# Attention on 32 memory slots, then a mixture of experts: the queries are transposed on TensorE, the first two batches are worked on in halves

## The chip, the cores and the metric

The kernel runs on one core of one Trainium2 chip, in float32. The metric is the device time of one execution in microseconds (us). One program does everything: attention first, then the expert network, then the output.

## The reference

There are 8 batches, 8 heads, 576 positions, head size 64, and M = 32 memory slots for each head. The attention works on those slots:

```python
a = exp(phi - phi.max(axis=2)); a /= a.sum(axis=2) + 1e-9        # phi: [8, 8, 576, 32]
k_m = einsum('bhsm,bhsd->bhmd', a, k)                           # 32 pooled keys for each head
v_m = einsum('bhsm,bhsd->bhmd', a, v)
scores = q @ k_m.T / 8; attn = softmax(scores)                  # over the 32 slots
x = (attn @ v_m) as rows of [8 * 576, 512]                      # heads side by side
```

The expert network routes all 4608 rows to 32 slots (8 experts with 4 slots each) by `logits = x @ moe_phi`:

```python
d = softmax(logits, over the 4608 rows); slot_input = d.T @ x
for e in range(8):
    slot_out[e] = relu(slot_input[e] @ w1[e]) @ w2[e]           # w1[e]: 512x1024, w2[e]: 1024x512
c = softmax(logits, over the 32 slots); out = c @ slot_out      # [4608, 512]
```

So 33 MB of q, k, v and phi are read, then 33.5 MB of w1 and w2, and 9.4 MB are written. No row of `slot_input` is final before the last row of all batches has its logits.

## The kernel before

**How the order comes about.** All work is handed to `Plan.add(engine, cost, fn, r=, w=, ...)` with an estimated duration. `Plan.order` then places the operations one after another on five queues (TensorE `PE`, VectorE `DVE`, ScalarE `ACT`, GpSimd `POOL`, and `SP`, which issues every DMA), by these estimates and by the priorities that `plan.at` sets. What comes out is a fixed order on each engine; on the chip each engine goes through its own queue in order, and waits where a semaphore is not there yet. `Slots` are pools of buffers inside one large SBUF tile, the `arena`; a tile of a pool becomes free when its last user is done.

**The attention** goes over four pairs of batches (`bp`), and in a pair over `c` = 0 to 3, two heads each.

- `pool_phi` loads phi of one batch, takes its maximum over the positions (DVE L511, a transposition on PE L519, DVE L524, a broadcast on PE L533, ACT L544), subtracts it on POOL (L549), takes exp on ACT (L555), adds up the nine position blocks on POOL (L562, four instructions that halve the blocks), folds the two halves of the partitions with one small product on PE (L572, with `maskhp`), and takes the reciprocal on DVE (L579, L580).
- `pool_kv` loads k and v of the batch and forms k_m and v_m in PSUM (`kvbank`) with 72 products (L599), whose operands are 64 rows by 32 columns, so that eight tiles of the array work side by side. ACT scales them (L615, L622). The keys are written into zeroed tiles `kps` in two 32-row blocks, and four transpositions on PE (L635) turn them into `kd`; L640, L645 and L662 do the same for the values and multiply them by moe_phi, which gives `vpb`.
- `q_blocks`: DVE transposes q in blocks of 32x32, straight from the loaded tile, in two instructions for each batch (L700). This is why the keys are needed in two blocks: each score is a sum of two products over 32 rows.
- `scores`: 8 products for each `c` (L716, 64x64 tiles, 288 columns) into `scbank`; DVE transposes them back (L730).
- `softmax` of each `c`: DVE maximum (L746), POOL subtraction (L751), ACT exp (L756), DVE sum (L761), ACT, DVE reciprocal (L770), POOL product (L774), DVE transposition (L777); `logits` on PE (L785). When the four `c` of a pair are done, DVE writes the pair's logits `L` (L955).
- `route` of each pair forms that pair's share of `slot_input` (L803 to L922; on PE L810, L821, L849, L875, L881, L909).

When the last pair is routed, DVE joins the four shares and writes `SIM`, the `slot_input` (L969 to L1000). POOL clears the tile `hT` for the hidden layer (L1046) shortly before that.

**The experts.** w1 and w2 come in 32 tiles of 1 MB each (`load_w`). Their buffers `ws` are 19 slots that lie over the arena: a slot can be loaded only when all attention buffers under it are done. PE multiplies (L1064 with w1, L1113 with w2), then come a sum `sr` (L1194 to L1207), 36 products L1220 with the rows' weights `cT`, copies on ACT and DVE (L1229, L1231), and 12 stores of 768 KB (L1239).

**Loads and fillers.** SP issues all loads at L458, in one queue; `FIRST` lists the first nine in order. phi, k and v have two buffers each (`phis`, `kvs`), q has two (`qs`, outside the arena). PE also gets filler products that compute nothing needed (L476, `NWARM` 40 of them at most in the first 25 us of the plan, `NTAIL` 12 around the end of the attention).

## Time and profile before

| | |
|---|---|
| three runs | 224.52, 222.32, 224.25 us, median 224.25 |
| the profiled execution | 221.83 us, of which the span from first to last instruction is 220.1 |
| busy in the span | PE 172.5 us, DVE 135.5, POOL 86.7, ACT 71.4 |
| moved by DMA | 76.45 MB, mean 347 GB/s |
| fillers on PE (L476) | 92 instructions, 25.4 us busy |
| pairs done (start of L955) | first at 62.7 us, last at 135.8 |

A float32 product is two MATMUL instructions in the trace, a transposition on PE is one. A row of the windows gives, for a stretch of the span, the busy time of each engine with the number of instructions, then the granted TensorE clock (1.00 is full speed), the mean busy share of the DMA engines (which reads up to 1.09 when they are saturated) and the GB/s that they moved. A row of the timeline gives start, length, engine, line and operation, and in brackets how long the engine had been idle and what released it.

### The profile page before, as it was taken

The numbers are of one execution on the slowest core, as the hardware profiler recorded it, in microseconds if no ns is written. First come the engines' busy times: TensorE is split into PE (matmuls) and PEld (weight loads), VectorE is DVE, ScalarE is ACT, GpSimd is POOL, SyncE is SP. The second block draws the span as 40 slices with busy tenths as digits, with TensorE's granted clock in tenths as the row PEclk, the third lists the DMA queues.
The fourth block names the chain that finished last, engine by engine and source line by source line (L and its number), as shares of the span: only waits on it lengthen the run. The fifth ranks groups of instructions, "written<-read, shape, count | busy, mean of one in ns | idle before, by whom it ended". The sixth has DMA issues, their size and how long they took to land.

```text
span 220.1 us, 5624 instructions
## 1 busy us (share of the span) xinstructions
PE 172.5 (78%) x2418; PEld 105.3 (48%) x2418; DVE 135.5 (62%) x230; ACT 71.4 (32%) x182; POOL 86.7 (39%) x85
## 2 busy tenths in 40 slices
PE   8997977695798988598988799629999975599400
PEld 6676745354564654356654387415554340065100
DVE  6825048969459999879658965499102860268500
ACT  2041234542516626337342340201002331168400
POOL 6298019596934992999623641030000000000000
PEclk9999999979699999999969999976999999769755
DMA  6999999999999999999596493999999998049997
GB/s 215 383 395 390 380 392 381 390 380 390 385 388 389 388 406 380 389 392 406 194 410 212 188 420 102 401 350 327 395 413 410 408 409 320 3 179 411 415 415 295
DMA packets 27881, 76.45 MB, mean 347 GB/s; under 512 B 1744, under 2 KB 5840, under 8 KB 27856
## 3 DMA queue, kind: packets, MB, share of 16 engines
q1 hardware_dynamic: 27856, 76.09, 91.1%
q8 instruction: 19, 0.31, 0.6%
q14 instruction: 6, 0.05, 0.1%
HBM read 66.65 MB, written 9.44 MB: 346 GB/s over the span
## 4 chain that ended last, share of the span: by engine, by line
PE 41%; DMA 22%; DVE 14%; POOL 9%; issue 5%; ACT 2%; SPq 1%; DVEq 0%; POOLq 0%
DMA top<-in_q_dram 10%; DMA arena<-in_moe_w_dram 9%; PE bank L1064 7%; PE kvbank L476 6%; PE bank L785 5%; PE scbank L716 4%; PE bank L1220 4%; PE kvbank L599 3%; DMA out_dram<-arena 3%; DVE arena L700 3%; POOL arena L774 3%; POOL arena L562 3%; PE bank L849 2%; PE kvbank L1113 2%; POOL arena L751 2%
## 5 line engine op out<-in xcount | busy, mean ns | idle before, releaser
L549 POOL TENSOR_TENSOR arena<-arena 128x1152 f32<-128x1152 f32 x8 | 21.0, 2632 | 16.0 <-ACT arena L544 13.3
L476 PE MATMUL kvbank<-ones 128*128 128x256 f32 x92 | 25.4, 419 | 2.2 <-ACT arena L622 1.1
L700 DVE STREAM_TRANSPOSE arena<-top 128x1152 f32<-128x1152 f32 x16 | 21.7, 1361 | 7.1 <-DMA top<-in_q_dram 7.1
L774 POOL TENSOR_TENSOR arena<-arena,ssm 128x576 f32<-128x576 f32 x16 | 18.5, 1162 | 15.6 <-DVE ssm L770 15.5
L562 POOL TENSOR_TENSOR arena<-arena 128x128 f32<-128x128 f32 (+2 forms) x32 | 23.4, 731 | 2.3 <-ACT arena L555 0.3
L716 PE MATMUL scbank<-arena 64*64 64x288 f32 x256 | 21.6, 433 | 3.0 <-DVE arena L730 2.5
L785 PE MATMUL bank<-arena 128*128 128x288 f32 x64 | 21.4, 464 | 2.6 <-DVE arena L777 2.6
L751 POOL TENSOR_TENSOR arena<-arena,smx 128x576 f32<-128x576 f32 x16 | 18.4, 1158 | 11.5 <-DVE smx L746 11.5
L599 PE MATMUL kvbank<-arena 64*32 64x128 f32 x1152 | 20.2, 273 | 2.2 <-issue 1.5
L476 PEld LDWEIGHTS kvbank<-ones 128*128 128x128 f32 x92 | 18.1, 207 | 6.7 <-issue 1.6
L511 DVE TENSOR_REDUCE arena<-arena 128x128 f32<-128x1152 f32 x8 | 17.0, 2138 | 5.6 <-DMA arena<-in_phi_dram 5.6
L599 PEld LDWEIGHTS kvbank<-arena 64*32 64x32 f32 x1152 | 16.2, 106 | 6.3 <-issue 3.9
L1064 PE MATMUL bank<-arena,SIM 128*32 128x256 f32 x256 | 16.4, 421 | 3.4 <-DVE SIM L1000 3.4
L1113 PE MATMUL kvbank<-arena 128*32 128x512 f32 x128 | 15.6, 598 | 2.9 <-DMA arena<-in_moe_w_dram 2.9
L730 DVE STREAM_TRANSPOSE arena<-scbank 128x576 f32<-128x576 f32 x16 | 12.2, 765 | 8.9 <-PE scbank L716 8.9
L785 PEld LDWEIGHTS bank<-arena 128*128 128x128 f32 x64 | 12.1, 206 | 8.1 <-DVE arena L777 3.8
L1220 PE MATMUL bank<-sr,cT 128*128 128x512 f32 x36 | 13.2, 505 | 3.1 <-DVE sr L1207 1.4
L1231 DVE COPY arena<-bank 128x512 f32<-128x512 f32 x18 | 11.8, 691 | 4.7 <-DMA out_dram<-arena 2.4
L777 DVE STREAM_TRANSPOSE arena<-arena 128x576 f32<-128x576 f32 x16 | 12.1, 758 | 3.8 <-POOL arena L774 3.7
L716 PEld LDWEIGHTS scbank<-arena 64*64 64x64 f32 x256 | 9.0, 137 | 10.8 <-DVE arena L730 4.5
L756 ACT ACTIVATE arena<-arena 128x576 f32<-128x576 f32 x16 | 11.0, 688 | 8.4 <-POOL arena L751 8.4
L1064 PEld LDWEIGHTS bank<-arena,SIM 128*32 128x32 f32 x256 | 8.6, 121 | 10.7 <-DVE SIM L1000 3.6
(104 smaller groups left out, 234.4 us busy)
## 6 DMA issues: line engine op xcount, KB each, us to landing
arena<-in_moe_w_dram SPq DMA_DIRECT2D x32, 1024.0 KB, 9.9
top<-in_q_dram SPq DMA_DIRECT2D x8, 1152.0 KB, 13.8
arena<-in_k_dram SPq DMA_DIRECT2D x8, 1152.0 KB, 11.2
arena<-in_v_dram SPq DMA_DIRECT2D x8, 1152.0 KB, 13.6
out_dram<-arena SPq DMA_DIRECT2D x12, 768.0 KB, 7.6
arena<-in_phi_dram SPq DMA_DIRECT2D x8, 576.0 KB, 8.7
arena<-in_moe_phi_dram SPq DMA_DIRECT2D x1, 64.0 KB, 4.8
```

Source lines behind the costliest of these rows:

```text
L476: lambda: nc.tensor.matmul(warm.ap, ones, ones.unsqueeze(1).to_broadcast([P, 2, P]), start=True, stop=True,),
L549: lambda: nc.gpsimd.tensor_tensor(ph(), ph(), mb.ap.unsqueeze(2).to_broadcast([P, C, J, M]), op=ALU.subtract),
L562: plus = lambda o, x, y: nc.gpsimd.tensor_tensor(o, x, y, op=ALU.add)
L599: nc.tensor.matmul(acc.ap[M * c: M * c + M, a, : 2 * D], ph()[h0: h0 + HALF, c, j, :], kv()[h0: h0 + HALF, :, c, j * D: j * D + D], start= ...
L700: nc.vector.transpose(qT.ap.rearrange("p (i u y) -> p u i y", i=2, y=Y), qt.ap[:, h * QT_SZ: h * QT_SZ + QT_SZ].rearrange("p (u i x) -> p ...
L716: nc.tensor.matmul(scb.ap[HALF * g: HALF * g + HALF, a, :JY], kb[g].ap[h0: h0 + HALF, i, c].rearrange("p r m -> p (r m)"), qT[g][c // 2].a ...
L751: lambda: nc.gpsimd.tensor_tensor(exv(), exv(), bc(mx), op=ALU.subtract),
L774: lambda: nc.gpsimd.tensor_tensor(exv(), exv(), bc(sm), op=ALU.mult),
L785: nc.tensor.matmul(lp.ap[:, :JY], vpb.ap[:, h, :], aT.ap[:, a * JY: (a + 1) * JY], start=(h == 0), stop=(h == H - 1),)
L1064: nc.tensor.matmul(hb.ap[NS * j: NS * j + NS, :256], SIM.ap[:, 2 * i + c, NS * e: NS * e + NS], wv[:, c, 256 * j: 256 * j + 256], start=(e ...
L1113: nc.tensor.matmul(pacc.ap[NS * x: NS * x + NS, 0, :DM], hT()[:, 4 * t + 2 * i + j, NS * e: NS * e + NS], wv[:, j, t, :], start=(e == 0 an ...
L1220: lambda po=po, i=i, ct=cT[bp, j0]: nc.tensor.matmul(po.ap[:, :DM], ct.ap()[:, i * P: i * P + P], sr.ap, start=True, stop=True),
```

## The change

1. **q on PE.** `turn_q` replaces the DVE transpositions: for each batch and each half of the heads, three groups of three 128x128 tiles are transposed on PE (L565; in the middle group one tile is made of two products with 64 columns, L557) into the free columns of `kvbank`, and ACT copies each group to SBUF (L572, 128x384). The pool `b_q` has two tiles, one in each bank of `kvbank`.
2. **Plain keys, 64x32 tiles.** The full 64 rows of q now lie on the partitions, so `kd` holds plain keys (2 transpositions L714 for each batch instead of 4), `kps` needs no zeros, and `scores` has 16 products (L787) with tiles of 64x32 and 128 or 160 columns, none of which adds up. DVE transposes the scores back in two instructions (L804).
3. **phi sums on PE.** The POOL additions and L572 are gone; `summed` has 36 products of 2 columns for each batch (L648).
4. **Halves.** For the first pair, `units` is 2: phi, k, v and q are loaded in halves of the heads, and the whole chain runs for each half.
5. **Three buffers** for phi and for k and v.
6. **Clearing on DVE.** `hT` is cleared by DVE (L1125), with `SIM` as its input as before.
7. The fillers write to `scbank` instead of `kvbank` and have 192 columns instead of 256 (L478).

```diff
-    kps = stack([2, KP_W], 2)
+    kps = stack([2, 2, D], 2)
-    trees = stack([C, 4, M], 1)
-    phis = stack([PHI_SZ], 2, fifo=True)
-    kvs = stack([KV_SZ], 2, fifo=True)
+    phis = stack([PHI_SZ], 3, fifo=True)
+    kvs = stack([KV_SZ], 3, fifo=True)
...
-    FIRST = ["phi0", "phi1", "mphi", "q0", "k0", "v0", "q1", "k1", "v1"]
+    FIRST = [
+        "phi0.0", "phi1.0", "k0.0", "v0.0", "k1.0", "v1.0", "mphi", "q0.0", "q1.0",
+        "phi0.1", "phi1.1", "k0.1", "v0.1", "k1.1", "v1.1", "q0.1", "q1.1",
+    ]
...
+        def turn_q(self, h):
+            for x in range(3):
+                tp = b_q.tile()
...
+                        if n == JH:
+                            for c in range(2):
+                                nc.tensor.matmul(
+                                    o[HALF * c: HALF * c + HALF],
+                                    qv[:, 2 * h + c, (J - 1) * D: J * D],
+                                    ident, start=True, stop=True,
+                                    tile_position=(0, HALF * c),
+                                )
+                        else:
+                            c, j = (0, n) if n < JH else (1, n - JH - 1)
+                            nc.tensor.transpose(
+                                o, qv[:, 2 * h + c, 2 * j * D: 2 * (j + 1) * D], ident
+                            )
+                add(PE, 0.36, f, r=[qt.part(h), ident_b], w=[tp], also=[qT])
+                add(
+                    ACT, act(3 * P),
+                    lambda x=x, tp=tp: nc.scalar.copy(qT.ap[:, 3 * P * x: 3 * P * (x + 1)], tp.ap),
...
+                for j in range(J):
+                    for c in range(c0, c1):
+                        nc.tensor.matmul(
+                            sp.ap[M * c: M * c + M, :2], ph()[:, c, j, :], maskhp,
+                            start=(j == 0), stop=(j == J - 1), tile_position=(0, M * c),
+                        )
...
+        units = 2 if bp == 0 else 1
...
-    add(POOL, 2.0, lambda: nc.gpsimd.memset(hTb.ap, 0.0), r=[SIM], w=[hTb])
+    add(DVE, 2.4, lambda: nc.vector.memset(hTb.ap, 0.0), r=[SIM], w=[hTb])
```

The order moves with it. **The start of SP's queue** (all DMAs; `arena` holds phi, k, v and the weights, `top` holds q), before:

```order
L458 DMA arena<-in_phi_dram 128x4x288 x2
L458 DMA arena<-in_moe_phi_dram 128x4x32
L458 DMA top<-in_q_dram 128x4x576
L458 DMA arena<-in_k_dram 128x4x576
L458 DMA arena<-in_v_dram 128x4x576
L458 DMA top<-in_q_dram 128x4x576
L458 DMA arena<-in_k_dram 128x4x576
L458 DMA arena<-in_v_dram 128x4x576
```

and now:

```order
L457 DMA arena<-in_phi_dram 128x2x288 x2
L457 DMA arena<-in_k_dram 128x2x576
L457 DMA arena<-in_v_dram 128x2x576
L457 DMA arena<-in_k_dram 128x2x576
L457 DMA arena<-in_v_dram 128x2x576
L457 DMA arena<-in_moe_phi_dram 128x4x32
L457 DMA top<-in_q_dram 128x2x576 x2
L457 DMA arena<-in_phi_dram 128x2x288 x2
```

Half of phi, k and v of both batches now stands ahead of any q.

**PE around the first pooled keys** (`kvbank<-arena` are the pooling products, `kvbank<-ident,top` the transpositions of q, `bank<-maskhp` the phi sums, `kvbank<-ones` fillers), before:

```order
L599 MATMUL kvbank<-arena 32x128 x72
L476 MATMUL kvbank<-ones 128x256 x2
L572 MATMUL bank_64<-maskhp,arena 128x2
L476 MATMUL kvbank<-ones 128x256 x5
L635 MATMUL bank_63<-ident,arena 128x4x32 x4
L640 MATMUL bank_62<-ident,arena 128x128
L572 MATMUL bank_64<-maskhp,arena 128x2
```

and now:

```order
L648 MATMUL bank_63<-maskhp,arena 32x2 x18
L673 MATMUL kvbank<-arena 32x128 x36
L648 MATMUL bank_64<-maskhp,arena 32x2 x18
L565 MATMUL kvbank<-ident,top 128x128 x4
L557 MATMUL kvbank<-ident,top 64x128 x2
L565 MATMUL kvbank<-ident,top 128x128
L714 MATMUL bank_62<-ident,arena 128x64 x2
L722 MATMUL bank_63<-ident,arena 128x64
L673 MATMUL kvbank<-arena 32x128 x36
```

The fillers have given way to phi sums and q, and each group asks for another tile shape than the one ahead of it.

**DVE around `SIM`** (`st` is the common denominator, `cmx` the first step of the row softmax for the output), before:

```order
L990 TENSOR_SCALAR st<-st 128x32
L991 RECIPROCAL st<-st 128x32
L998 TENSOR_TENSOR arena<-bank_63,arena 128x128
L999 TENSOR_TENSOR arena<-arena 128x128
L1000 TENSOR_TENSOR SIM<-arena,st 128x32x4
L1136 TENSOR_REDUCE cmx_96<-L_89 128x9
```

and now:

```order
L1069 TENSOR_SCALAR st<-st 128x32
L1070 RECIPROCAL st<-st 128x32
L1077 TENSOR_TENSOR arena<-bank_62,arena 128x128
L1078 TENSOR_TENSOR arena<-arena 128x128
L1079 TENSOR_TENSOR SIM<-arena,st 128x32x4
L1125 MEMSET arena 128x2304
L1215 TENSOR_REDUCE cmx_96<-L_89 128x9
```

The clearing of `hT` stands behind `SIM` on DVE, and no longer on POOL.

More of the change, by code (lines that the diff above doesn't have):

```diff
@@ L312 @@
     banks = [psum.tile([P, 512], F32, name=f"bank{i}") for i in range(4)]
-    b_kv = Slots([kvbank])
+    b_kv = Slots([kvbank], [(10, 1)])
+    b_q = Slots([kvbank[:, i, P:] for i in range(2)], [(10, 1), (10, 1)])
+    b_acc = Slots([kvbank], [(10, 1)], (b_kv, b_q))
     b_m = Slots(banks[:3], [(i, 1) for i in range(3)])
@@ L324 @@
     PHI_SZ, KV_SZ = C * J * M, 2 * C * J * D
-    Q_SZ, QT_SZ = C * J * D, C * J * D // 2
-    KP_W = R * (P + Y)
+    Q_SZ, QT_SZ = C * J * D, J * P
+    JH = J // 2
+    POS = [j // 2 if j % 2 == 0 else (J + 1) // 2 + j // 2 for j in range(J)]
     EX_SZ = PC + JN
@@ L417, in f @@
         nc.vector.memset(ones, 1.0)
-        for a in kps.aps:
-            nc.vector.memset(a, 0.0)
         for a in sexs.aps:
@@ L531, in f, with scores, blocks @@
+    def scores(c, pair, ex):
+        scb = b_s2.tile()
+        def blocks(s):
+            n = JH + (s == c % 2)
+            b = 0 if c % 2 == 0 else JH + 1 - s
+            pos = 0 if s == 0 else J - n
+            return n, b, pos
         def f():
             for a in range(2):
-                nc.tensor.matmul(
-                    t1.ap[HALF * a: HALF * a + HALF, :P],
-                    mh.ap[:, a: a + 1].to_broadcast([P, HALF]),
-                    ident,
-                    start=True,
-                    stop=True,
-                )
@@ L612, in pool_kv, with turn @@
+        add(
+            PE, 0.6, f,
+            r=[*(x.qT[c // 2] for x in pair), *(x.kd.part(x.part(c)) for x in pair)],
+            w=[scb], also=[ex],
+        )
+        def turn(s):
+            n, _, pos = blocks(s)
+            nc.vector.transpose(
+                ex.ap[:, c * PART: (c + 1) * PART].rearrange("p (a x) -> p a x", a=2)[
+                    :, :, pos * Y: (pos + n) * Y
+                ],
+                scb.ap[:, s, : 2 * n * Y].rearrange("p (a x) -> p a x", a=2),
             )
@@ L626, in pool_kv @@
-        add(ACT, 2 * act(P) + 2 * act(D), f, r=[acc, rs], w=[kp, vm])
-        tp, tv = b_m.tile(), b_m.tile()
-        kd, vT = kbs.tile(), vTs.tile()
-        def f():
-            o = tp.ap.rearrange("p (i c r m) -> p i c r m", i=2, c=C, r=R)
-            for i in range(2):
-                for r in range(R):
-                    nc.tensor.transpose(o[:, i, :, r, :], kp.ap[:, i, r * P: r * P + P], ident)
-        add(PE, 4 * 0.11, f, r=[kp, ident_b], w=[tp], also=[kd])
-        add(
-            PE, TP,
-            lambda: nc.tensor.transpose(tv.ap[:, :P], vm.ap.rearrange("p a d -> p (a d)"), ident),
-            r=[vm, ident_b], w=[tv], also=[vT],
-        )
@@ L680, in pool_kv @@
-        for r in range(R):
-            add(ACT, act(H * NS), lambda f=f, r=r: f(r), r=[vpp], w=[vpb.part(R * g + r)])
-        return vm, kd
-    def load_q(b):
-        qt = qs.tile()
-        load(
-            lambda: qt.ap.rearrange("p (c x) -> p c x", c=C), rows(q, b), H * S * D * 4, qt,
-            pri=first(f"q{b}"),
-        )
-        return qt
-    def q_blocks(qt):
-        halves = []
-        for h in range(2):
-            qT = qTs.tile()
-            def f(h=h, qT=qT):
-                nc.vector.transpose(
-                    qT.ap.rearrange("p (i u y) -> p u i y", i=2, y=Y),
-                    qt.ap[:, h * QT_SZ: h * QT_SZ + QT_SZ].rearrange("p (u i x) -> p u i x", i=2, x=Y),
-                )
-            halves.append((qT, f))
-        return halves
@@ L708, in scores @@
[L708 to L735 removed]
+            turn(0)
@@ L737, in softmax @@
+            turn(1)
+        add(DVE, 2 * dve(PART // 2), f, r=[scb], w=[ex.part(c)])
     def softmax(c, ex):
@@ L791, in f, with route @@
                 )
-        add(PE, 0.96, f, r=[aT, vpb], w=[lp])
-    def route(bp, ex, vm):
+        add(PE, 0.96, f, r=[aT, *(vpb.part(4 * u + x) for x in range(4))], w=[lp])
+    def route(bp, ex, pair):
         dm1, dmh, df = dm1s.tile(), dmhs.tile(), dfs.tile()
@@ L915, in f @@
                     )
-        add(PE, 0.6, f, r=[wtb, *vm], w=[sip])
+        add(PE, 0.6, f, r=[wtb, *(x.vm for x in pair)], w=[sip])
         if bp == NSEG - 1:
@@ L950 @@
             plan.at(bp + 0.25 * c, 15)
-            scores(c, qT, kb, ex)
+            scores(c, pair, ex)
             aT = softmax(c, ex)
-            logits(c, aT, vpb, lp)
+            logits(c, aT, vpb, pair[0].part(c), lp)
         add(
```

444 lines of the change are left out of this document (254 added, 190 removed).

## Prediction

> **What bounds the kernel now.** I read the page first, for the span and the bytes that move, then the windows, then the chain that ended last.
>
> ```profile
> span 220.1 us, 5624 instructions
> PE 172.5 (78%) x2418; PEld 105.3 (48%) x2418; DVE 135.5 (62%) x230; ACT 71.4 (32%) x182; POOL 86.7 (39%) x85
> GB/s 215 383 395 390 380 392 381 390 380 390 385 388 389 388 406 380 389 392 406 194 410 212 188 420 102 401 350 327 395 413 410 408 409 320 3 179 411 415 415 295
> ```
>
> No engine is busy for the whole span. The DMA row has three parts: about 390 GB/s without a gap for the first 104 us, holes from there to 140 us, then 410 GB/s until the weights end. Each slice is 5.5 us.
>
> ```profile
> 0.00:104.00 104.00, 86.15 (x1607) 58.87 (x1611) 75.63 (x115) 41.34 (x104) 70.37 (x70) 0.97 1.03 380
> 104.00:140.00 36.00, 31.53 (x343) 20.70 (x329) 25.06 (x45) 10.78 (x37) 14.29 (x15) 0.95 0.70 266
> 140.00:188.00 48.00, 39.31 (x464) 18.09 (x447) 21.60 (x52) 8.46 (x23) 2.02 (x1) 0.93 0.96 373
> ```
>
> The holes say how much there is to win on the transfers. At 380 GB/s the middle row would lose 36 x (1 - 266/380) = 10.8 us less, and the slices of 350 and 327 (143 to 154 us) another 1.9 against their neighbours' 410: **12.7 us**. What makes the holes, the chain and SP's queue tell.
>
> ```profile
> 147.32 0.30 DVE SIM L1000
> 147.67 10.18 PE bank L1064 x144
> ...
> 168.59 18.81 DMA arena<-in_moe_w_dram
> ...
> 187.44 1.11 PE kvbank L1113 x8
> ```
>
> ```profile
> 147.75 21.26 SPq L458 DMA_DIRECT2D arena<-in_moe_w_dram  x14
> ```
>
> When SIM is written, at 147.6 us, 14 of the 32 weight tiles are not yet issued: every slot is full, and only L1064, which needs SIM, frees them. From then on there is a fixed stretch: 39.8 us until the last tile has landed (187.4), then 32.7 us of output, whose code is not changed. So **end = SIM + 72.5 us**, as long as slots, and not bytes, are short; the gain ends at 12.7 us, where the holes are gone. The profiled execution took 221.83 us, 1.7 more than its span. I sum against it; the median of the runs, 224.25, is 1.1% higher, which I take as the spread of executions.
>
> So the question is when SIM comes: the engines' work up to there.
>
> ```profile
> 62.70:94.90 32.20, 27.27 (x558) 17.10 (x561) 29.99 (x45) 13.55 (x38) 20.43 (x18) 1.00 1.05 391
> 94.90:120.00 25.10, 22.61 (x372) 14.45 (x365) 18.75 (x33) 10.68 (x33) 15.30 (x15) 0.93 0.85 322
> ...
> 135.80:147.60 11.80, 5.58 (x64) 3.71 (x63) 8.00 (x17) 1.80 (x8) 2.02 (x1) 0.90 0.89 324
> sum 147.60, PE 120.68 PEld 81.58 DVE 105.99 ACT 53.09 POOL 86.67; mean PE 20.11 PEld 13.60 DVE 17.66 ACT 8.85 POOL 14.45
> ```
>
> ```profile
> sum 147.60, PE 25.36 PEld 18.06; mean PE 4.23 PEld 3.01
> ```
>
> ```profile
> 135.83 0.48 DVE L955 STREAM_TRANSPOSE L<-bank 128x288 f32<-128x288 f32 x1 [1.90 <-PE bank L785]
> ```
>
> The columns are PE, PEld, DVE, ACT, POOL. DVE has the most work, 106 us, and is 93% busy in the second pair (29.99 of 32.20). PE's 120.7 hold 25.4 of fillers (the second fence), so its own work is 95.3, and POOL has 86.7. The last logits are done at 135.8; the 11.8 us behind them are the last pair's routing.
>
> **The change part by part.** The rows for the prices:
>
> ```profile
> L700 DVE STREAM_TRANSPOSE arena<-top 128x1152 f32<-128x1152 f32 x16 | 21.7, 1361 | 7.1 <-DMA top<-in_q_dram 7.1
> L562 POOL TENSOR_TENSOR arena<-arena 128x128 f32<-128x128 f32 (+2 forms) x32 | 23.4, 731 | 2.3 <-ACT arena L555 0.3
> L716 PE MATMUL scbank<-arena 64*64 64x288 f32 x256 | 21.6, 433 | 3.0 <-DVE arena L730 2.5 <-DVE prs L579 0.5
> L730 DVE STREAM_TRANSPOSE arena<-scbank 128x576 f32<-128x576 f32 x16 | 12.2, 765 | 8.9 <-PE scbank L716 8.9
> L635 PE MATMUL bank<-ident,arena 128*128 128x128 f32 x32 | 5.9, 317 | 1.4 <-ACT arena L615 1.4
> L654 ACT COPY arena<-bank 128x512 f32<-128x512 f32 x8 | 4.7, 587 | 6.2 <-PE bank L635 6.2
> L572 PE MATMUL bank<-maskhp,arena 128*128 128x2 f32 x16 | 2.6, 235 | 0.0
> ```
>
> ```profile
> 168.26 1.20 PE L1170 MATMUL bank<-ident,arena 128*128 128x128 f32 x9
> 107.85 1.08 PE L875 MATMUL bank<-rep,arena 128*128 128x32 f32 x8
> 15.78 2.24 PE L599 MATMUL kvbank<-arena 64*32 64x128 f32 x144
> 139.17 1.65 PE L849 MATMUL bank<-arena 64*32 64x288 f32 x36 [1.16 <-DVE m L969]
> ```
>
> *q.* DVE loses 21.7 us. PE gains 16 rounds (8 batches, 2 halves) of eight transpositions and one tile of 64-column products. Nine transpositions took 1.20 us, so 16 x 1.13, 18 us, is the low end. The odd tile is four instructions of another shape; L875 gives 0.54 us for four, and two changes of shape (priced below) add 0.4, in place of one transposition: at most 16 x 1.75 = 28. I take **24**, since that tile stands in the middle of each round. ACT gains 48 copies of 384 columns, each under L654's 0.59 us for 512: at most 28 us.
>
> *phi sums.* POOL loses 23.4. PE gains 8 x 72 instructions, 128x32 tiles, two columns. Low: L599's 2.24 / 144 = 15.6 ns each, 9 us; high: a quarter of L875's 135 ns (four tiles side by side), 34 ns, 19 us. I take 18 ns, near L599, whose weights are also 32 columns wide: **10.4**. L572's 2.6 goes.
>
> *Scores.* PE had 21.6. Now 16 x 32 instructions of 144 columns on average. L599's 15.6 ns has 128 columns: 16 x 0.56 = 9 us; L849's 45.8 ns has 288: 16 x 1.47 = 23.5. By columns between them, 0.73 each, 11.7: **10 us less** (from -12.6 to +1.9). DVE's transposition in two pieces costs at most twice L955's 0.48 against 0.765: +3.1.
>
> *Keys.* Half of L635: **-2.5** on PE. DVE no longer clears kps.
>
> *Halves.* Small products run twice for the first pair: **+2** on PE at most. What it brings is the start. The first pooling product ran at 15.78; the halves cut the two maxima ahead of it, the subtraction and the exp by half (below: 2.1, 1.3 and 0.6), and the loads ahead of v by 3 MB, 8 us at 380 GB/s. The shorter saving counts: start at about **11 us**. PE's second pooling group now waits for q's first half, which lands later than its k and v; that is inside this start.
>
> ```profile
> L511 DVE TENSOR_REDUCE arena<-arena 128x128 f32<-128x1152 f32 x8 | 17.0, 2138 | 5.6 <-DMA arena<-in_phi_dram 5.6
> L549 POOL TENSOR_TENSOR arena<-arena 128x1152 f32<-128x1152 f32 x8 | 21.0, 2632 | 16.0 <-ACT arena L544 13.3 <-issue 2.7
> L555 ACT ACTIVATE arena<-arena 128x1152 f32<-128x1152 f32 x8 | 9.3, 1164 | 7.9 <-POOL arena L549 7.9
> ```
>
> *Third buffers.* Worth nothing by themselves: the loads already ran at 380 GB/s up to 104 us. They take room under one early weight slot, which is covered as long as SIM, and not an early slot, is what the loads wait for.
>
> *Clearing.*
>
> ```profile
> 144.38 2.02 POOL L1046 MEMSET arena<- 128x2304 f32 x1 [11.25 <-PE bank L909]
> 144.53 1.90 DVE L990 TENSOR_SCALAR st<-st 128x32 f32<-128x32 f32 x1
> ...
> L1148 DVE TENSOR_SCALAR csm<-csm 128x9 f32<-128x9 f32 x4 | 0.7, 174 | 0.1
> ```
>
> L990 stands on the chain to SIM. It took 1.90 us and ended with POOL's clearing; L1148, the same operation, takes 0.17. With the clearing behind SIM on DVE this goes: **-1.7 us**, and the 2 us that DVE now spends there lie beside L1064's 10 us.
>
> *The sum.* DVE comes to about 106 - 21.7 + 3.1 = 87, POOL to 61, ACT to at most 81. PE, the fullest now, had 95.3 - 5.6 = 90 us up to the last logits, and gets 24 + 10.4 - 2.6 - 10 - 2.5 + 2 = 21: **111 us**. How dense can it run? It was 85% busy in the second pair and 90% in the third (22.61 of 25.10), when it was not the fullest; now others wait for it, so I take 92%: 11 + 111.3/0.92 = 132.0 us for the last logits instead of 135.8. SIM: 132.0 + 11.8 - 1.7 = 142.1, which is 5.5 us earlier, and the time is **216.3**; I write 217, as the runs lie above the profiled one.
>
> The change of shape needs a price of its own.
>
> ```profile
> 118.36 1.24 PE L785 MATMUL bank<-arena 128*128 128x288 f32 x4
> 133.69 2.10 PE L785 MATMUL bank<-arena 128*128 128x288 f32 x8
> ```
>
> Four logit products between other shapes took 1.24 us, eight in a row 2.10: each separate group pays 0.19. Up to SIM, PE's order has 88 stretches of one tile shape before and 143 now, 55 more, 10.5 to 11 us. My q term holds 6 of it.
>
> [...]
>
> **The rivals.**
> 1. *Every change of shape is paid, no change in time.* PE's work is 116.3 instead of 111.3, the last logits come at 11 + 126.4 = 137.4, SIM at 147.5: **221.7**. For it: the L785 rows. Against: groups that wait for ACT or DVE anyway hide it.
> 2. *PE is cheap, and the bytes bound.* With the low ends PE has 99 us; below 105 at 92% the last logits come before 124.8 and the holes are gone: **209.1**. For it: PE's gaps in the last pair are filled with fillers. Against: three terms must be low together.
> 3. *PE waits for ACT, slower.* A q group can start only when the copy of the second last has left its bank, ACT works in order, and pooling products use the same two banks. Everything on PE queues behind a waiting group: scores, logits, pooling of the next pair. If 12 of the 48 groups stand behind an exp of L555 (1.16 us), PE loses 14 us: last logits at 145.9, SIM at 156.0, **230.2**. It turns slower than 1% when the mean group waits 0.16 us more than in my 8% of idle (7.7 us over 48). For it: ACT's work grows by half. Against: ACT is 55% busy even so.
>
> **How the numbers follow.** Forecast 0.44 (211 to 219.5), rival 1 0.16, rival 2 0.17, rival 3 0.23. About 1% is what a measurement of this kernel tells from no change. Faster: 0.44 + 0.17 = 0.61; same 0.16; slower 0.23. The range takes in rival 2 and reaches to rival 3: 208.5 to 230.5. The upper ends of sums and scores together (PE at about 130) lie beyond it.
>
> **What would show it.** Up to SIM: PE 117 us without fillers, DVE 87, POOL 61. L565 with L557 about 24, L648 10, L787 12. L955's last at 132, L1079 at 142, L1069 at 0.2 us. Still 13 to 14 weight tiles after SIM and 72.5 us from SIM to the end. Wrong, if PE's work is off by more than 8 us, if PE idles for ACT L572, or if the first pooling (L673) starts after 13 us.

## The result, and the profile after

The changed kernel takes **266.5 us** (median of four runs, 264.0 to 268.5), the kernel before 224.0 in the same session: a ratio of 1.187, interval 1.174 to 1.201, where 217 us was forecast. Some executions of all these kernels, the profiled one of the changed kernel among them, show a lower granted clock (0.852 there, 0.859 to 0.869 in its other three runs) and a longer time, and the ratios and their intervals leave those out. The profiled execution took 268.5 us, the longest of the four, so its totals are the upper end.

The rows of the page after, as they answer to those of before:

```profile
span 266.7 us, 7639 instructions
PE 207.8 (78%) x3396; PEld 136.4 (51%) x3396; DVE 118.3 (44%) x237; ACT 93.0 (35%) x250; POOL 62.3 (23%) x54
PEclk9997989986988659977977999995569999958975
GB/s 202 372 382 384 349 228 363 276 380 229 228 91 72 353 345 398 309 2 0 288 414 407 44 325 389 284 166 260 315 326 407 412 408 407 251 0 275 414 414 313
q8 instruction: 26, 0.43, 0.7%
```

The transfers now have holes from 33 us on (a slice is 6.7 us). The granted TensorE clock is low in far more slices (its mean over the span is 0.852, before 0.916). The last row will matter: q8 is a queue whose kind the page calls "instruction", here with 26 packets and 0.43 MB, where the page of before had this:

```profile
q8 instruction: 19, 0.31, 0.6%
```

When SIM is written after: DVE's timeline, and SP's behind it.

```profile
179.62 0.48 DVE L1034 STREAM_TRANSPOSE L<-bank 128x288 f32<-128x288 f32 x1 [1.33 <-PE bank L865]
191.06 0.18 DVE L1069 TENSOR_SCALAR st<-st 128x32 f32<-128x32 f32 x1
192.14 0.29 DVE L1079 TENSOR_TENSOR SIM<-arena,st 128x128 f32<-128x128 f32 x1
```

```profile
192.57 21.86 SPq L457 DMA_DIRECT2D arena<-in_moe_w_dram  x14
```

SIM comes at 192.1 us instead of 147.3, and 266.7 - 192.1 = 74.6 us follow it, 72.7 before. So 44.8 of the 46.6 us by which the span grew were lost **ahead of SIM**. There, the windows of after and one of before (us, then busy time of PE, PEld, DVE, ACT, POOL, granted clock, DMA share, GB/s), and the fillers alone in the last fence:

```profile
0.00:30.00 30.00, 25.33 (x307) 20.54 (x308) 7.69 (x19) 8.87 (x26) 8.38 (x15) 0.94 0.97 341
30.00:163.80 133.80, 108.02 (x2412) 77.04 (x2411) 62.89 (x120) 58.16 (x163) 45.84 (x33) 0.86 0.71 256
163.80:192.10 28.30, 21.36 (x220) 14.81 (x218) 15.98 (x35) 7.60 (x25) 8.09 (x8) 0.80 0.72 266
sum 192.10, PE 154.71 PEld 112.39 DVE 86.55 ACT 74.62 POOL 62.31; mean PE 51.57 PEld 37.46 DVE 28.85 ACT 24.87 POOL 20.77
```

```profile
30.00:123.90 93.90, 77.22 (x1420) 48.82 (x1420) 74.91 (x118) 41.24 (x113) 63.48 (x57) 0.95 0.98 364
```

```profile
sum 192.10, PE 17.38 PEld 13.77; mean PE 17.38 PEld 13.77
```

These middle rows are the stretch with hardly any fillers (0.04 us of them before, 1.05 after). PE is busy for 108.02 of 133.80 us there, 81%; before it was 77.22 of 93.90, 82%. PE is busy 40% longer there and no denser, at a clock of 0.86 instead of 0.95. The groups that pay, after:

```profile
L673 PE MATMUL kvbank<-arena 64*32 64x128 f32 x1152 | 31.8, 323 | 12.4 <-issue 11.3
L565 PE MATMUL kvbank<-ident,top 128*128 128x128 f32 x128 | 25.5, 302 | 12.2 <-ACT arena L572 5.1
L787 PE MATMUL scbank<-arena 64*32 64x160 f32 (+1 forms) x512 | 14.2, 311 | 0.0
L557 PE MATMUL kvbank<-ident,top 128*64 128x128 f32 x64 | 7.3, 307 | 0.0
L648 PE MATMUL bank<-maskhp,arena 128*32 128x2 f32 x576 | 8.0, 175 | 2.7 <-ACT arena L635 2.7
```

The first row is the surprise. The pooling products L673 are the 1152 instructions that were L599, with the same operands, but 11.3 us of idle time stand ahead of them put down to "issue": TensorE waits for nothing that the profile shows. Before, it was 1.5 us:

```profile
L599 PE MATMUL kvbank<-arena 64*32 64x128 f32 x1152 | 20.2, 273 | 2.2 <-issue 1.5 <-ACT arena L555 0.7
```

PE's timeline after, at the longest of these stops:

```profile
52.71 0.78 PE L648 MATMUL bank<-maskhp,arena 128*32 128x2 f32 x72 [1.85 <-ACT arena L635]
53.42 1.49 PE L673 MATMUL kvbank<-arena 64*32 64x128 f32 x82
59.05 1.95 PE L673 MATMUL kvbank<-arena 64*32 64x128 f32 x62 [4.13 <-issue]
```

It stops in the middle of one group of 144, with no wait in the program. I counted PE's instructions from the start of the program (each matmul has its weight load, 3396 of both by the page, so they count twice). The six stops of over 0.6 us up to SIM stand at numbers 1729, 2241, 3009, 3777, 4289 and 4546: five are 193 plus a multiple of 256, the last is one past it. And 0.43 MB / 26 is 16.5 KB, 6830 instructions / 26 is 263. The grid 193, 449, 705 and so on has 26 points in these 6830 instructions and 19 in the 4876 of before, as many as there are packets: **one packet for 256 instructions**, by this count, and these six stops stand on that grid.

The trace's records give the start of each packet. Below, the moment at which PE crossed into the 256 before, when the next packet moved, and when PE went on:

```
kernel   crossing of   at us    packet           next stop at  goes on   crossing to going on
after    1473          52.91    56.61 to 57.70   1729          59.05     6.1 us
after    3521          108.72   111.54 to 112.60 3777          114.06    5.3
before   449           23.24    26.09 to 27.18   705           28.69     5.5
```

In these rows, with the loads running, the packet moves 2.8 to 3.7 us after PE has crossed into the 256 ahead of the stop, and PE goes on 5.3 to 6.1 us after the crossing. That PE waits for the packet is my reading of them, and the runs below test it. From 52.71 us on, 72 + 82 matmuls, 308 instructions, were used up in 2.2 us. Before, only four of the 14 runs of 256 up to 131 us were used up in less than 5.3 us (in 4.6 to 5.0): its two such stops add up to 1.5 us.

Behind the two longest of these stops the granted clock is lower. Three windows after show it for one (the clock stands ahead of the DMA share):

```profile
108.00:114.00 6.00, 2.89 (x145) 2.18 (x144) 4.74 (x9) 1.12 (x4) 2.66 (x3) 1.00 0.65 259
114.00:120.00 6.00, 4.65 (x22) 3.21 (x22) 0.29 (x1) 2.45 (x8) 0.82 (x1) 0.68 0.01 3
120.00:126.00 6.00, 6.00 (x62) 4.00 (x61) 2.40 (x5) 2.12 (x6) 1.83 (x1) 0.75 0.00 0
```

```profile
SPq L457 <- PE kvbank L565: 28.4, 2, 25.2
```

PE stood from 110.9 to 114.1, put down to "issue", and from 114.9 to 116.1 for ScalarE (L696); from 116.2 to 123.0 the granted clock was 0.50 (by the clock records). At the stop of 54.9 to 59.1 us, which has no second wait beside it, a stretch at 0.50 begins at 58.1 and lasts 6.8 us. And PE's lateness makes the hole in the loads: SP stood for 25.2 us, up to 125.7, until L565 had read the q buffer that the next load of q was to fill. The stretches at 0.50 last 3.41, 6.83 or 10.24 us up to 180 us. In the last 3.41 us ahead of the one at 116.2 PE was busy for 0.90 us, and for 0.19 ahead of the one at 58.1. What brings the clock down is not shown: no run changes that alone.

### The profile page after: what moved, and what is told of

It is laid out like the page before. It is cut to its first block, busy times and chain, and to the rows that moved or that the text cites. A ratio compares the mean times of both kernels' runs of the same rounds, so it can differ in the third digit from the quotient of the medians.

```text
span 266.7 us, 7639 instructions
## 1 busy us (share of the span) xinstructions
PE 207.8 (78%) x3396; PEld 136.4 (51%) x3396; DVE 118.3 (44%) x237; ACT 93.0 (35%) x250; POOL 62.3 (23%) x54
## 4 chain that ended last, share of the span: by engine, by line
PE 61%; DMA 11%; ACT 9%; issue 8%; DVE 5%; POOL 2%; POOLq 0%; DVEq 0%; ACTq 0%
PE kvbank L673 12%; PE kvbank L565 8%; DMA arena<-in_moe_w_dram 7%; PE bank L1143 6%; PE bank L865 6%; PE scbank L478 4%; ACT arena L572 4%; PE bank L929 3%; PE scbank L787 3%; PE bank L1299 3%; DMA out_dram<-arena 3%; PE kvbank L557 2%; PE kvbank L1192 2%; PE bank L648 2%; PE bank L747 2%
## 5 line engine op out<-in xcount | busy, mean ns | idle before, releaser
L673 PE MATMUL kvbank<-arena 64*32 64x128 f32 x1152 | 31.8, 323 | 12.4 <-issue 11.3
L565 PE MATMUL kvbank<-ident,top 128*128 128x128 f32 x128 | 25.5, 302 | 12.2 <-ACT arena L572 5.1
L673 PEld LDWEIGHTS kvbank<-arena 64*32 64x32 f32 x1152 | 26.2, 124 | 15.4 <-issue 13.8
L626 POOL TENSOR_TENSOR arena<-arena 128x1152 f32<-128x1152 f32 (+1 forms) x10 | 21.4, 2142 | 51.7 <-ACT arena L619 51.7
L572 ACT COPY arena<-kvbank 128x384 f32<-128x384 f32 x48 | 21.2, 483 | 24.4 <-PE kvbank L565 21.3
L565 PEld LDWEIGHTS kvbank<-ident,top 128*128 128x128 f32 x128 | 14.8, 145 | 21.7 <-ACT arena L572 8.5
L804 DVE STREAM_TRANSPOSE arena<-scbank 128x320 f32<-128x320 f32 (+1 forms) x32 | 13.5, 461 | 25.6 <-PE scbank L787 24.9
L478 PE MATMUL scbank<-ones 128*128 128x192 f32 x62 | 17.4, 431 | 1.1 <-DVE ones L418 1.1
L584 DVE TENSOR_REDUCE arena<-arena 128x128 f32<-128x1152 f32 (+1 forms) x10 | 17.2, 1740 | 1.2 <-DMA arena<-in_phi_dram 1.2
L841 DVE TENSOR_REDUCE ssm<-arena 128x18 f32<-128x576 f32 x16 | 11.8, 736 | 9.7 <-ACT arena L836 9.7
L478 PEld LDWEIGHTS scbank<-ones 128*128 128x128 f32 x62 | 13.8, 253 | 2.1 <-DVE ones L418 1.1
L787 PE MATMUL scbank<-arena 64*32 64x160 f32 (+1 forms) x512 | 14.2, 311 | 0.0
L599 DVE TENSOR_REDUCE pmh<-bank 128x2 f32<-128x128 f32 (+1 forms) x10 | 2.8, 283 | 24.9 <-PE bank L592 24.9
```

Source lines behind the costliest of these rows:

```text
L478: lambda: nc.tensor.matmul(warm.ap, ones, ones[:, :96].unsqueeze(1).to_broadcast([P, 2, 96]), start=True, stop=True,),
L565: nc.tensor.transpose(o, qv[:, 2 * h + c, 2 * j * D: 2 * (j + 1) * D], ident)
L572: lambda x=x, tp=tp: nc.scalar.copy(qT.ap[:, 3 * P * x: 3 * P * (x + 1)], tp.ap),
L626: lambda: nc.gpsimd.tensor_tensor(ph(), ph(), mb.ap[:, c0:c1].unsqueeze(2).to_broadcast([P, c1 - c0, J, M]), op=ALU.subtract,),
L673: nc.tensor.matmul(acc.ap[M * c: M * c + M, a, : 2 * D], ph()[h0: h0 + HALF, c, j, :], kv()[h0: h0 + HALF, :, c, j * D: j * D + D], start= ...
L787: nc.tensor.matmul(scb.ap[x: x + Y, s, n * Y * a: n * Y * a + n * Y], pair[g].kd.ap[h0: h0 + HALF, a, c, :], pair[g].qT[c // 2].ap.rearran ...
```

## Experiments

The working behind each: time up to SIM, split for PE into its own work (busy time times granted clock), fillers likewise (time in which the two overlap is shared between them), busy time lost to a clock below 1, stops (idle time of over 0.6 us, put down to "issue", at a boundary of 256 instructions), and all other idle time. These are from the profiled execution of each kernel. The time is the median of all timed runs; the ratio is to the kernel before on the same chip, and a comparison of two rows goes by it.

```
kernel                                  time   ratio [95%]           SIM    own   fill  clock stops other idle
before                                  224.0                        147.3  91.5  24.1   5.1   1.5  25.1
after                                   266.5  1.187 [1.174, 1.201]  192.1 115.8  16.4  22.6  13.4  23.9
e1  after, sums on POOL                 249.5  1.117 [1.107, 1.126]  176.7 111.7  18.2  13.9   5.2  27.7
e2  after, sums in wide matmuls         259.7  1.165 [1.154, 1.176]  185.3 129.3  16.1  13.2   3.2  23.6
e3  before + sums on PE                 246.7  1.106 [1.096, 1.115]  169.3  93.3  21.4  13.7  24.7  16.2
e4  before + sums in wide matmuls       228.7  1.026 [1.019, 1.033]  152.2 102.7  19.8  10.8   5.3  13.7
e5  before + q on PE                    243.1  1.086 [1.069, 1.103]  166.4 105.4  17.3  10.8   8.5  24.4
e7  e1, q in other banks                243.9  1.088 [1.076, 1.101]  167.2 108.1  18.2  15.8   7.3  17.7
e8  e1, q's copies on two engines       267.7  1.198 [1.173, 1.223]  191.2 111.4  16.2  23.1   6.2  34.2
e9  before + clearing on DVE            224.7  0.998 [0.993, 1.003]  147.8  90.3  23.4   8.9   0.7  24.5
e10 e9 + third buffers                  228.0  1.021 [1.015, 1.028]  152.0  89.0  24.7  10.4   7.5  20.5
e11 e9 + halves                         229.5  1.029 [1.022, 1.037]  152.4  95.2  19.4  10.6   0.0  27.3
e12 e3, sums held back                  245.9  1.099 [1.092, 1.106]  170.1  91.6  21.7  19.1  18.6  19.0
e13 e3, light loads                     235.3  1.048 [1.037, 1.059]  159.6  92.6  21.3  13.1  16.3  16.2
e14 after, light loads                  254.3  1.121 [1.108, 1.133]  176.2 116.1  15.3  14.3   6.3  24.3
e15 before, light loads                 224.3  1.002 [0.998, 1.007]  149.6  89.6  23.7  11.2   0.0  25.1
e16 e5, q in other banks                229.1  1.024 [1.009, 1.040]  152.1 103.2  18.0   8.0   8.8  14.0
e17 after, q in other banks             261.8  1.169 [1.151, 1.187]  184.1 115.2  15.2  18.6  20.1  14.9
```

The clock column of the same work moves by some 4 to 6 us between executions (before, e9 and e15 have 5.1, 8.9 and 11.2), so only larger differences are read from it. e4's profile ran at a granted clock of 0.92 up to SIM and 0.88 over its span, its other three runs at 0.92 to 0.93 over theirs, which stands in its column. Lines of the experiments' profiles are off by a few from those quoted above. The expectations of e13 to e15 count a stop from the start of the instruction ahead of it, which adds some 0.3 us to each.

### e1 to e4: the phi sums

e1 undoes the sums alone; e2 leaves them on PE with fewer instructions:

```diff
 # e1, in summed()
-    for j in range(J): for c in range(c0, c1): nc.tensor.matmul(sp..., ph()[:, c, j, :], maskhp, ...)
+    # POOL: the tree of additions of before, then one matmul of es with maskhp
 # e2, in summed()
-                    for c in range(c0, c1):
-                        nc.tensor.matmul(sp.ap[M * c: M * c + M, :2], ph()[:, c, j, :], maskhp, ...)
+                    nc.tensor.matmul(sp.ap[:2, :n], maskhp, ph()[:, c0:c1, j, :], ...)
+    # DVE copies the two rows, one small matmul turns them
```

> The changed kernel with one part undone: the phi sums are a tree of additions on POOL again and one small matmul, q stays on PE. Theory F (code fetch): TensorE stands still where it crosses from one run of 256 of its instructions to the next before the next 16 KB instruction packet has landed, because sums (144 instructions) and pooling (288) stand next to each other and are used up in about 3.5 us; the stops are followed by windows of half clock. Without the sums the idle time of the pooling group put down to issue falls from 11.3 us to under 4, the clock-weighted loss before SIM from some 17 us to under 10, and the time from 266 to 232-248. Theory A (waits for ScalarE's copies of q and the bank that they share with pooling): only the sums' own 8 us of PE go, 256-262, and the stops in pooling stay. Theory T (the PE work of q itself was mis-sized): 256-262 as well, with the pooling's stops whatever they are.

> The changed kernel with the phi sums still on TensorE, but with the two-column mask as the stationary tile and 128 columns of phi moving: 9 matmuls in place of 36 for a batch, plus one small copy on DVE and one small transposing matmul. The busy time for the sums stays about the same (some 8 us for 8 batches), the instructions for them fall from 144 to some 40 a batch. Theory F (code fetch): the stops in pooling fall from 11.3 us to under 5 and the time to 238-250. Theories A and T: the number of instructions does not matter, 262-270.

e3 and e4 put the two forms of the sums into the kernel before, and nothing else of the change:

```diff
 # e3, in pool_phi() of the kernel before; e4 as in e2
-        add(POOL, ..., f, r=[pt], w=[es, tr])
+            for j in range(J): for c in range(C):
+                nc.tensor.matmul(sp.ap[M * c: M * c + M, :2], ph()[:, c, j, :], maskhp, ...)
+        add(PE, 1.4, f, r=[pt, maskhp_b], w=[sp], also=[rs])
```

> The kernel before with one part of the change: the phi sums as 36 small matmuls a batch on TensorE in place of the POOL tree and one matmul. q stays on DVE, no copies of q on ScalarE. Theory F (code fetch): stops at instruction boundaries appear in the pooling (1.5 us of issue before becomes 8-14) and the time rises to 234-246. Theories A and T: there are no copies of q and no shared bank, so only the 5.4 us of added PE work can show, against a POOL relieved by some 17 us: 220-230.

> As the run before it, but with 9 matmuls of 128 moving columns a batch in place of 36 of two. Same PE time within 2 us, a third of the instructions. Theory F: the stops are mostly gone, 222-230, at least 8 us below its neighbour. Theories A and T: within 3 us of its neighbour.

The pair e3 and e4 is the cleanest result. First PE's timeline of e3 at one stop and the pooling's group, then the groups of pooling and sums of e4:

```profile
42.26 0.78 PE L562 MATMUL bank<-maskhp,arena 128*32 128x2 f32 x72
42.97 1.37 PE L590 MATMUL kvbank<-arena 64*32 64x128 f32 x80
48.55 0.86 PE L590 MATMUL kvbank<-arena 64*32 64x128 f32 x20 [4.21 <-issue]
```

```profile
L590 PE MATMUL kvbank<-arena 64*32 64x128 f32 x1152 | 25.6, 313 | 24.9 <-issue 24.7
```

```profile
L598 PE MATMUL kvbank<-arena 64*32 64x128 f32 x1152 | 21.6, 283 | 2.0 <-issue 2.0
L562 PE MATMUL bank<-arena,maskhp 128*2 128x128 f32 x144 | 18.4, 284 | 4.9 <-issue 2.9 <-ACT arena L555 2.0
```

In e3 the sums are 6.6 us of PE work and cost 23.6 us (246.7 against 223.2): 24.7 us of stops stand in the pooling, seven of them at a boundary. In e4 the same sums are 18.4 us of PE work, with 18 matmuls a batch where e3 has 72, and the kernel is **18 us faster** than e3. In this pair more work in fewer instructions wins, as theory F had it, and A and T fall for this part. I had taken 8 us for the wide form; it is 18.4, 128 ns a matmul with 128 moving columns (18.4 / 144), where those with two columns take 11.5 (6.6 / 576).

In the full change the sums are worth 17 us (e1, 1.5 us above the range of theory F), with 8.2 us fewer stops and 8.7 us less lost clock. The wide form there (e2) takes 10 us of stops away and adds 13.5 us of work, so it came out 10 us above the range of theory F and 2 us below that of A and T. And e1 still leaves 26 us that are not the sums.

### e5, e6: q, and what is left

```diff
 # e5: after, with
+    sums as in e1; units = 1; phis, kvs: 2 buffers
 # e6: after, with sums as in e1 and
-        tp = b_q.tile(); nc.tensor.transpose(...); nc.scalar.copy(...)
+        nc.vector.transpose(qT..., qt...)      # keys and scores in their old form too
```

> The kernel before with q transposed on TensorE, copied by ScalarE, and keys and scores in 64x32 tiles, and with the clearing on DVE; the phi sums stay on POOL, the first pair is not halved, two input buffers. With the phi sums back on POOL the changed kernel still took 249.5 us, 26 more than the kernel before. Theory Q (q's work on TensorE is paid in full, with its waits): this run is the same 26 us slower, 244-252. Theory H (the halves and third buffers, by the order of the loads, cost the rest): 222-232.

> The changed kernel with q on DVE and keys and scores as before, and with the phi sums on POOL: what is left of the change is the first pair in halves, three input buffers and the clearing on DVE. Theory Q: 217-226, near the kernel before, 2 us better by the clearing. Theory H: 238 or more.

Both theories were half right. q alone costs 8.6%, and halves with third buffers cost as well: of e6's four runs (233.2 to 239.9 us) only the one of 233.2 can be compared, beside 222.7 to 225.8 for the kernel before, so the size of this is rough. e10 and e11 take these two apart below. Where e5 loses, PE's waits:

```profile
PE kvbank L563 <- ACT arena L709: 4.2, 3, 1.6
PE kvbank L686 <- issue: 4.1, 3, 2.4
PE kvbank L563 <- ACT arena L570: 3.8, 7, 1.0
PE kvbank L563 <- issue: 3.0, 1, 3.0
```

q's groups (L563) wait for the scaling of the pooled values (L709) and for the last copies of q (L570), all in the one pair of banks, kvbank; the rest is stops.

### e7, e8, e16, e17: the banks and the copies

```diff
 # e7, e16, e17 (on e1, e5 and the full change)
-    b_q = Slots([kvbank[:, i, P:] for i in range(2)], [(10, 1), (10, 1)])
-    b_acc = Slots([kvbank], [(10, 1)], (b_kv, b_q))
+    b_acc = Slots([kvbank], [(10, 1)], (b_kv,))
     b_m = Slots(banks[:3], [(i, 1) for i in range(3)])
+    b_q = b_m
 # e8 (on e1)
-                    ACT, act(3 * P), lambda ...: nc.scalar.copy(...)
+                    *((DVE, dve(3 * P)) if (x + h) % 2 else (ACT, act(3 * P))), lambda ...: ...
```

> As the run with the phi sums back on POOL (249.5 us), but q's groups are written to the three general PSUM banks in place of the pooling's bank pair. There the groups waited 6.2 us for the scaling of the pooled sums (L712) and 3.8 us for the copies of q (L573). Theory A (the shared bank pair and its waits make the loss): the first of these waits goes and what stood behind it moves up, 236-243. Theory Q (the work itself): 246-252, the waits turn up at another place.

> As the run with the phi sums back on POOL (249.5 us), but half of the copies of q run on DVE in place of ScalarE. Theory A (TensorE waits for ScalarE's copies): the waits for L573 and L712 halve, 240-246. Theory Q: 246-252.

> q on TensorE alone (243.1 us), but its groups are written to the three general banks and not to the pooling's pair. In the changed kernel with the phi sums on POOL that took the time from 249.5 to 243.9. If the two add up: 235-240, still slower than the kernel before, which leaves q's work and its stops as the rest. If the banks cost only together with the halves: 241-245.

> The changed kernel in full (266.5 us), but q's groups are written to the three general PSUM banks in place of the pooling's pair. With q alone the same edit took 14 us (243.1 to 229.1), with halves, third buffers and q 5.6 us (249.5 to 243.9). If the bank pair is a term of its own: 253-261. If in the full change the stops for code decide anyway: 262-268, with TensorE's waits for ScalarE gone and its stops longer.

With q alone the banks are nearly everything: e16 is **14 us** below e5, its other idle time falls from 24.4 to 14.0 us, and of the 19 us that q cost only 5 are left, though PE's own work is the same 103 to 105 us. That was more than I expected. The edit does two things at once: q's groups no longer share banks with the pooling, and they have three banks to go round in, not two. No run separates these. With halves and third buffers beside it (e7, 0.9 us above theory A's range) the same edit is worth 5.6 us. In the full change (e17) it brings 266.5 to 261.8, at the edge of what separate runs can tell; PE's waits there:

```profile
PE kvbank L673 <- issue: 18.4, 7, 4.6
PE bank L592 <- DVE arena L584: 3.2, 2, 1.6
```

The 9.8 us of waits of L565 for ScalarE are down to 0.2 and the stops have grown from 13.4 to 20.1 us. That one wait had hidden the other is my reading of these two numbers.

e8 went the wrong way, by 18 us. Its waits say how:

```profile
PE kvbank L566 <- ACT arena L714: 10.4, 7, 2.2
...
ACT arena L573 <- DVE arena L573: 13.3, 5, 5.8
DVE arena L573 <- ACT arena L573: 6.1, 6, 1.6
```

The copies on the two engines wait for each other. They read the same pair of banks and their order follows the tiles, and DVE works in order behind the softmax. Moving half of the copies to DVE did not shorten the wait for the bank: behind the scaling of the pooled values q's groups stood for 10.4 us, in e1 for 6.2.

### e9 to e11: clearing, third buffers, halves

```diff
 # e9, on the kernel before
-    add(POOL, 2.0, lambda: nc.gpsimd.memset(hTb.ap, 0.0), r=[SIM], w=[hTb])
+    add(DVE, 2.4, lambda: nc.vector.memset(hTb.ap, 0.0), r=[SIM], w=[hTb])
 # e10, on e9
-    phis, kvs = ... 2 ...
+    phis, kvs = ... 3 ...
 # e11: e6 with
+    phis, kvs: 2 buffers
```

> The kernel before with the clearing of hT on DVE behind SIM and nothing else. By the prediction's term: L1069's forerunner L990 takes 0.2 us in place of 1.9 and the time falls by 1.7 us, 0.8%. A rival: the 2 us that DVE spends on the clearing stand ahead of the first hidden rows, no change.

> The kernel before with the clearing on DVE and with three buffers for phi and for k and v; no halves. The run with halves and third buffers together (q and sums as before) was 233 to 240 us. Theory B (third buffers let the loads of a later pair go ahead of what is needed next): 230-238. Theory H (the halves do it: more instructions and groups on PE at the start): 220-225, no more than the clearing alone.

> The kernel before with the clearing on DVE and the first pair in halves of the heads, two buffers. Theory B: 218-224. Theory H: 230-238.

The clearing does what was forecast on its own line (L990 takes 0.18 us), but the ratio is 0.998, interval 0.993 to 1.003: no difference that can be told, and the 1.7 us lie at the interval's very end. Third buffers cost 2.4% and halves 3.2% against e9 (ratios of 1.021 and 1.029 against 0.998), each alone; both times lie between the ranges of the two theories. e11 also carries the changed order of the first loads and the changed fillers, which no run has alone. One wait of each:

```profile
PE bank L810 <- issue: 4.2, 1, 4.2
```

```profile
PE kvbank L673 <- ACT arena L620: 6.2, 4, 2.9
```

The first is e10: one stop of 4.2 us, and another of 2.4 us. The loads ran at 380 GB/s up to 104 us without third buffers (before); with them the stops rise from 0.7 us (e9) to 7.5. The second is e11: no stops, but the pooling stands for the exp of phi (L620) on ScalarE. That these two waits are the whole of either loss is read from one profile each, not shown by a further run.

### e12 to e15: the packet and the loads

e12 has e3's instructions in another order; e13, e14 and e15 cut the loads of the last four batches in e3, in the full change, and in the kernel before:

```diff
 # e12
-        add(PE, 1.4, f, r=[pt, maskhp_b], w=[sp], also=[rs])
+        add(PE, 1.4, f, r=[pt, maskhp_b], w=[sp], also=[rs], slack=3.5)
 # e13, e14, e15: loads of phi, q, k, v
+    cut = lambda b: None if b < 4 else 16
-            lambda: pt.ap.rearrange("p (c x) -> p c x", c=C), rows(phi, b), ...
+            lambda: pt.ap.rearrange("p (c x) -> p c x", c=C)[:, :, :cut(b)], rows(phi, b)[:, :, :cut(b)], ...
```

> The same instructions as in the run of the kernel before with the phi sums on TensorE (246.7 us), but the sums are held back by 3.5 us in the order, so that they come after other matmuls and no longer stand right ahead of the pooling. Theory F (code fetch, 256 instructions at a time): the stops at the boundaries fall from 25 us before SIM to under 12, and the time to 228-238. A rival (the small products themselves, or the bank they are written to, make the pooling stand): 243-250.

e12 met neither expectation in full. The time stayed (245.9), and the stops fell only from 24.7 to 18.6 us, seven of them, at boundaries again. PE's timeline shows why:

```profile
94.29 2.25 PE L590 MATMUL kvbank<-arena 64*32 64x128 f32 x144 [0.52 <-ACT arena L554]
96.46 0.48 PE L562 MATMUL bank<-maskhp,arena 128*32 128x2 f32 x35
101.19 0.49 PE L562 MATMUL bank<-maskhp,arena 128*32 128x2 f32 x37 [4.25 <-issue]
```

The sums came right behind the pooling instead of ahead of it, and now it is they that stop. So it is not the pooling, its tile or its bank that stands: in e12 "issue" stands ahead of L562 for 9.1 us, L590 5.5, L626 2.5 and L707 1.6.

> The kernel before with the phi sums on TensorE (246.7 us), but the loads of phi, q, k and v for the last four of the eight batches bring only 16 of each row's elements, so that the DMA queues are nearly empty from the third pair on; instructions and order on every engine are the same, the results of those batches are not. With full loads TensorE went on about 6 us after it had crossed into a new run of 256 instructions (from 42.46 to 48.55 us, from 61.04 to 66.89), and the stops behind 62 us were 16.7 us. Theory F with load (the instruction packet waits behind data in the DMA engines): from the third pair on the 6 us become under 4 and the stops under 7 us; time 228-238. Theory F without load (the fetch takes that long anyhow): stops stay at 14 or more, 242-248.

> The changed kernel (266.5 us) with the same cut of the loads of the last four batches. Theory F with load: its stops behind 60 us fall from 10.8 us to under 4, half-clock time with them, 246-257. Theory F without load: 262-267. Theory Q (TensorE's own work and its waits for ScalarE make most of the loss) would still leave it over 246.

> The kernel before with the same cut, as the measure for the two others: it has hardly any stops (1.9 us), so 216-224; what the weights gain by coming earlier shows here.

The GB/s row of e13 (slices of 5.9 us; 3 to 200 GB/s from 47 to 100 us), and PE's timeline in the quiet stretch:

```profile
GB/s 218 389 392 389 339 389 223 388 127 20 180 143 55 18 3 200 44 328 139 223 6 322 362 224 378 323 178 250 413 408 408 408 411 378 16 66 411 412 415 302
```

```profile
73.91 0.78 PE L565 MATMUL bank<-maskhp,arena 128*32 128x2 f32 x72
74.62 1.09 PE L593 MATMUL kvbank<-arena 64*32 64x128 f32 x57
77.45 0.96 PE L593 MATMUL kvbank<-arena 64*32 64x128 f32 x31 [1.74 <-issue]
```

```
kernel  crossing of  at us   packet            goes on   crossing to going on
e3      1217         42.45   46.00 to 47.11    48.55     6.1 us  loads running
e3      1729         61.03   64.43 to 65.46    66.89     5.9     loads running
e13     1729         60.90   61.83 to 62.95    64.30     3.4     quiet
e13     2241         73.92   74.72 to 76.13    77.45     3.5     quiet
e13     3521         102.01  104.58 to 105.55  106.94    4.9     weights running
```

The packet itself takes the same 1.0 to 1.4 us; it *starts* 0.8 to 0.9 us after the crossing in the quiet rows, and 3.4 to 3.6 in those of e3, with the loads running. With the loads cut the stops get shorter: those behind 60 us fall from 14.6 to 6.2 us, and the time from 246.7 to 235.3, while the kernel before gains nothing by the same cut (e15). The full change goes from a ratio of 1.187 to 1.121, some 15 us, and its stops behind 60 us from 9.3 to 3.6 (e14). In the quiet rows 3.4 to 3.5 us are left; the 72 + 57 matmuls from 73.91 us on, 258 instructions, were used up in 1.8.

All profiles together say the same. They hold 73 stops of over 0.3 us at a boundary up to SIM. In eight of these the DMA engines were busy for less than 85% of the time between the crossing and the packet, and seven of the eight took 3.0 to 3.6 us from crossing to going on. Of the other 65, 60 took 4.9 to 7.7 us; five took only 3.5 to 4.4, so busy DMA engines did not always go with the longer time.

## Why the prediction was wrong

**Where it failed.** The step is "111.3/0.92": the sum took PE's time as busy time divided by a density, and the density as free to rise from 85 to 92%. It came to 81%, and the busy time itself grew with the lost clock. Three things did this that no term of the sum held:
- *Stops at boundaries of 256 instructions:* +11.9 us up to SIM (1.5 to 13.4). The prediction quoted pooling at 2.24 us for 144 matmuls and priced the sums beside it at 10.4 us, without a term for the number of their instructions. The profile before had a first sign of it: 19 instruction packets, and 1.5 us of issue within L599.
- *Clock:* +17.5 us (5.1 to 22.6), of which 4 to 6 can be chance. The sum had no clock in it.
- *Waits of q's groups in the shared banks:* 9.8 us for ScalarE (5.1 and 4.7), so that the other idle time hardly shrank: 25.1 us before, 23.9 after.

With +24.3 us of own work and 7.7 us fewer fillers, that makes +44.8. All three signs of being wrong that the prediction named came: PE's work off by more than 8 us (below), waits for L572, and a late first pooling.

**What held.** The terms of PE's work were right in sum: 21 us were forecast, 24.3 came at full clock. One by one, as busy time at the clock that was granted: L565 with L557 30.6 us (their rows add up to 32.8, but they overlap; 24 was forecast, to 28), L648 8.0 (10), L787 14.2 (12). The 28 was summed too low: nine transpositions at 1.20 us, less one at 0.13, and the odd tile with 0.54 and 0.4 are 2.0 us a round and not 1.75, so 32. PE's own busy time to SIM, 154.7 - 17.4 = 137.3 us, is 20 over the 117 forecast, about the clock's 22.6. DVE has 86.6 us (87), POOL 62.3 (61), ACT 74.6 (at most 81). The fixed stretch held: 14 weight tiles behind SIM, 74.6 us for 72.5. L1069 takes 0.18 us, as forecast, but is worth nothing that can be measured (e9).

**The start** failed its own mark: L673 first ran at 14.7 us, not 11, over the 13 that were named as the limit. Halves brought 1.1 us, and e11 shows that alone they cost 3.2% (against e9).

**"Third buffers: worth nothing"** was 2.4% off, on the slow side (e10 against e9).

**The rivals.** Rival 3 was the right direction and named the right place, the banks that q shares with pooling. That its 14 us are also what e16 takes back with q alone is chance: they were priced as 12 groups behind an exp, and in the full change the banks are worth 5 us (e17). It had 0.23, and the prediction leaned on ACT's 55% against it, though the wait is for a bank and not for a busy engine. Rival 1 stays open as a price: 24.3 us of growth lie between the 21 without it and its 26 (27 by the changed kernel's trace, which has 153 stretches of one tile shape up to SIM where the prediction counted 143), and the own work of unchanged code moves by 2 us between e9, e10, e15 and before. As an outcome it fell, as did rival 2, which needed 99 us. The case that came, with stops at boundaries of 256 instructions, was not among them, so the range missed.

**How the parts add up.** Alone, against the kernel before: sums +10.6%, q +8.6%, and against e9 halves +3.2% and third buffers +2.4%; 24.8% together, where the whole change costs 18.7%. They overlap; that a wait can hide a stop, as I read e17 (waits 9.8 to 0.2 us, stops 13.4 to 20.1), would be one reason. No version of these parts beat the kernel before; the nearest that has q on PE is e16, at +2.4% (0.9 to 4.0).

## What to carry to other kernels

Count instructions as well as busy time before moving work to TensorE: in these kernels a stop ended 3.0 us after the crossing at the least, and 4.9 to 7.7 in most cases while the loads ran, and a burst that had used up 308 instructions in 2.2 us stood for 4.1 (after, at 54.9 us). Fewer, larger matmuls that took longer won here: 144 with 18.4 us of busy time in e4 (228.7 us) against 576 with 6.6 us in e3 (246.7). An idle share on an engine is not room: up to SIM ACT was busy for 39% (74.6 of 192.1 us), and L565 still waited 9.8 us for it. So ask what each gap waits for, and whether the added work would wait for the same. Ask it of PSUM banks too: with q's groups out of the pair that the pooling writes, and three banks for two, 14 us were won with q alone (e16) and 5.6 in e7.

## What the hardware showed that I had not expected

- The page counts 26 packets of kind "instruction" on q8 after and 19 before, one for about 256 instructions of TensorE (6830 / 26 = 263, 4876 / 19 = 257). At the stops in the rows above, the next packet starts 0.8 to 0.9 us after the crossing with quiet queues and 2.6 to 3.7 with loads running; it moves for 1.0 to 1.4 us, and PE goes on 1.3 to 1.5 us after it has landed.
- The profile shows such a stop as idle time released by "issue", in the middle of a group without a wait; 24.7 us of one group in e3. The mark is the instruction's number, 193 plus a multiple of 256 in every stop of over 0.8 us put down to "issue" up to SIM in these kernels, give or take two.
- A change that raised PE's work by 11 us (e4 against before) cost 5.6 us, and one that raised it by 2 (e3) cost 24.
